# Column sums and the product with phi in 32-column strips, one transposed load of v dropped, three split pairs fewer, all steps reordered

## The chip, the cores and the metric

One core of one Trainium2 chip runs the whole kernel. The metric is the device time of one launch in microseconds (us), the median of three runs. TensorE (PE in the profile) multiplies, VectorE (DVE) and ScalarE (ACT) do the elementwise work, GpSimd (POOL) raises four small tiles to a power, and SyncE (SP) issues every DMA, one after the other, in its own queue.

## The reference

Two stages, everything in fp32. For each of B = 4 batches, column-normalised attention: q and k (5056 x 256) are divided by the norms of their columns, s = kn.T @ qn / tau is a 256 x 256 matrix, and a softmax over its rows gives a; the output of the stage is v @ a.

```
qn = q / (np.linalg.norm(q, axis=1, keepdims=True) + 1e-06)
kn = k / (np.linalg.norm(k, axis=1, keepdims=True) + 1e-06)
s = kn.transpose(0, 2, 1) @ qn / tau
a = softmax over the last axis of s
x = (v @ a).reshape(B * N, D)
logits = x @ phi                      # phi: 256 x 32
slot_input = softmax(logits, over rows).T @ x
h = relu(slot_input @ w1[e]);  slot_out = h @ w2[e]      # 8 experts, 4 slots each
out = softmax(logits, over the 32 slots) @ slot_out
```

The second stage is a soft mixture of experts over all 20224 rows at once: its first softmax runs over the rows of all four batches, so nothing of the experts can start before the last batch's logits are there.

## The kernel before, in words

**Pieces.** q and k come in 40 units of 1 MB (`raw0` to `raw39`, ten per batch, `load_qk`), v in 20 pieces of 1 MB (`v0` to `v19`, `load_v`). The logits need v transposed; each half (p, m) of a piece is either loaded in transposed form from a second copy in memory (`load_vt`, 0.5 MB, the pairs in the set `LT`) or turned on TensorE by four transposes per half of it (`turn`, L373, eight per pair (p, m)) and copied out by ScalarE (`turned`). Expert weights are 16 loads of 1 MB (`load_w1`, `load_w2`). The output is 20 MB, stored as ten halves of 0.5 MB and fifteen wholes of 1 MB (`store`).

**Scores.** Per unit there are four blocks j of 128 rows. `score` (L237) multiplies k.T q of a block into the batch's S, in one of two forms. Without a split the fp32 operands go in as they are: 4 matmul instructions per block (two per half m). If the pair (u, k) of blocks is in the set `SPLIT`, ScalarE copies it to a rounded high part (`cast`, L202), VectorE subtracts to get the low part (`low`, L207), and the block takes 6 cheaper instructions. ScalarE also squares every unit and VectorE adds the squares up (`add`), for the norms.

**Per batch**, in this order: `att_sums` folds the sum of squares to one tile a of 128 x 512; `att_cols` (L262) multiplies it by ones on TensorE so that the 512 column sums lie on partitions; `att_rn` copies them out on VectorE; `att_pow` takes the root on POOL; `att_norm` the reciprocal; `att_dg` (ScalarE) builds two diagonal matrices, and `att_row` (L296) multiplies ones by them so that each partition holds the row of q's norms; `att_scale`, `att_exp`, `att_turn`, `att_back` make a and its transpose; `att_phi` (L342) multiplies by phi; `att_m` (ScalarE) scales the product to M. With M, `logits` (L393) makes the logits of a piece of v straight from the transposed v, in four strips of 32 output partitions; `exps`, `weights`, `gather` do the row softmax and the weighted sum of v, group by group; `finish_fold` (L520) turns that sum by a matmul with the identity, and `finish_slots` multiplies by a.

**The end.** After the last `gather`, `last_slots` and `last_back` give the slot input; `up`, `relu`, `flip_h`, `down` are the experts, in two column halves h of the output. `down(r, h, f)` (L703) of the first half needs the four loads w2(k, 0), that of the second half the four w2(k, 1). `o_copy`, `o_fold`, `o_back` (L721 to L733) bring one half of the slot output into place, then `out_mul` (L740), `out_evict` and `store` make the output; the first ten stores are half ones.

**What sets the order.** Every call is entered in a list `plan`; the list `ORDER` then says, by hand, in which order all 992 calls are emitted. Each engine runs its own instructions strictly in that order, and SP its DMAs. All large tiles share 22 buffers of 1 MB; `HOME` says which tile lies in which buffer, so a load waits on SP for the last reader of the buffer's tile before it, and every load behind it waits too. `WAKE` dummy matmuls (L784) run on TensorE before the first data is there.

Of the kernel before, what the change touches and what calls it, by code (L numbers as in the profile page):

```python
# [8 lines left out]
F32 = mybir.dt.float32  # L9
F32R = mybir.dt.float32r  # L10
AF = mybir.ActivationFunctionType
ALU = mybir.AluOpType
# [8 lines left out]
WAKE = 9  # L21
# [4 lines left out]
SPLIT = {(u, 0) for u in range(1, NU) if u not in (1, 2, 3, 17, 20, 27, 31)} | {(u, 1) for u in (2, 5, 14, 24, 26, 27, 31, 33, 35, 37, 39)}  # L26
LT = {(p, 0) for p in (0, 2, 3, 4, 5, 6, 7, 8, 9, 11, 12, 13, 15, 18, 19)} | {(p, 1) for p in (0, 3, 6, 9, 12, 15)}
GR = {b: (3, 2) for b in range(B)}
HOME = {
# [74 lines left out]
def colnorm_attention_soft_moe(  # L104
# [157 lines left out]
    def att_cols(b):  # L262
        mp = bank(X0, f"nn{b}")
        a = sqs[b * UB][:, 0].rearrange("p x c -> p (x c)")
        for i in range(4):
            pe.matmul(mp[:, i : i + 1], a[:, P * i : P * i + P], ones[:, 0:1], start=True, stop=True)  # L266
# [829 lines left out]
```

## Time and profile before

| | |
|---|---|
| three runs | 276.80, 277.48, 277.49 us; median 277.48 us |
| the profiled execution | 277.06 us, of which 275.3 us are the span from first to last instruction |
| mean granted clock of TensorE | 0.939 of full |
| busy share of the span | PE 92%, DVE 86%, ACT 71%, POOL 3% |
| DMA | 111.44 MB moved, of it 90.08 MB read and 20.97 MB written |

The span is cut into 40 equal slices of 6.88 us in the page; a digit is the busy share of a slice in tenths. In the rows, a group is one line of the kernel on one engine, with its count, its total and the mean duration of one instruction. Matmuls overlap, so the time that a step takes on TensorE is read from start to start, as in the chain of waits, not from the mean duration of one.

### The profile page before, as it was taken

The numbers are of one execution on the slowest core, as the hardware profiler recorded it, in microseconds if no ns is written. First come the engines' busy times: TensorE is split into PE (matmuls) and PEld (weight loads), VectorE is DVE, ScalarE is ACT, GpSimd is POOL, SyncE is SP. The second block draws the span as 40 slices with busy tenths as digits, with TensorE's granted clock in tenths as the row PEclk, the third lists the DMA queues.
The fourth block names the chain that finished last, engine by engine and source line by source line (L and its number), as shares of the span: only waits on it lengthen the run. The fifth ranks groups of instructions, "written<-read, shape, count | busy, mean of one in ns | idle before, by whom it ended". The sixth has DMA issues, their size and how long they took to land.

```text
span 275.3 us, 6127 instructions
## 1 busy us (share of the span) xinstructions
PE 254.6 (92%) x2494; PEld 212.6 (77%) x2494; DVE 236.8 (86%) x349; ACT 195.5 (71%) x285; POOL 7.5 (3%) x12
## 2 busy tenths in 40 slices
PE   8999999999999999999999999999999988678730
PEld 8889998999998896997898978866555878457520
DVE  1599999999999999999999997887989879988630
ACT  3898989798899689899998783886416247353430
POOL 1000002000002000020000001000000000000000
PEclk9999999999999999999999999999999999855755
DMA  7999999999999999999999999999999789999995
GB/s 283 432 424 410 422 426 415 420 417 419 419 417 420 412 422 421 416 415 417 412 419 418 416 417 419 417 416 420 421 415 420 300 332 388 418 418 412 420 421 246
DMA packets 17883, 111.44 MB, mean 405 GB/s; under 512 B 2112, under 2 KB 2112, under 8 KB 6592
## 3 DMA queue, kind: packets, MB, share of 16 engines
q1 hardware_dynamic: 17856, 111.06, 98.0%
q8 instruction: 19, 0.31, 0.4%
q14 instruction: 8, 0.07, 0.1%
HBM read 90.08 MB, written 20.97 MB: 403 GB/s over the span
## 4 chain that ended last, share of the span: by engine, by line
PE 87%; DVE 6%; ACT 3%; issue 1%; DVEq 0%; ACTq 0%
PE S L255 46%; PE op_None L750 8%; PE L L403 7%; PE G L503 7%; PE vTp L376 6%; PE op L750 3%; PE O L711 2%; DVE o L774 2%; ACT o L772 2%; PE wake L787 2%; PE Mp L347 1%; PE nn L266 1%; DVE nat L630 1%; DVE cm L627 1%; PE sp L549 1%; PE gt L525 1%
## 5 line engine op out<-in xcount | busy, mean ns | idle before, releaser
L235 DVE TENSOR_TENSOR sq<-sq,sq 128x1024 f32<-128x1024 f32 (+1 forms) x61 | 81.3, 1356 | 8.4 <-ACT sq L220 8.0
L220 ACT ACTIVATE sq<-raw 128x2048 f32<-128x2048 f32 (+1 forms) x40 | 74.7, 1889 | 6.5 <-DMA raw<-in_qk_dram 4.8
L255 PE MATMUL S<-hl 128*128 128x256 f32 x516 | 71.5, 291 | 0.0
L255 PE MATMUL S<-raw 128*128 128x256 f32 (+1 forms) x296 | 66.9, 384 | 0.0
L255 PEld LDWEIGHTS S<-hl 128*128 128x128 f32 x516 | 65.2, 191 | 1.0
L255 PEld LDWEIGHTS S<-raw 128*128 128x128 f32 (+1 forms) x296 | 53.7, 192 | 8.1 <-issue 1.5
L209 DVE TENSOR_TENSOR hl<-raw,hl 128x1024 fp32r<-128x1024 f32 x43 | 51.6, 1219 | 0.7 <-ACT hl L204 0.7
L204 ACT CAST hl<-raw 128x1024 fp32r<-128x1024 f32 x43 | 44.0, 1048 | 6.1 <-PE S L255 2.5
L750 PE MATMUL op_None<-so,lg 32*128 32x256 f32 x240 | 26.4, 525 | 6.0 <-ACT o L772 4.1
L772 ACT COPY o<-op_None 128x512 f32<-128x512 f32 x30 | 15.8, 594 | 18.2 <-PE op_None L750 17.9
L750 PEld LDWEIGHTS op_None<-so,lg 32*128 32x128 f32 x240 | 19.6, 251 | 11.6 <-ACT o L772 6.3
L381 ACT COPY x<-vTp 128x512 f32<-128x512 f32 x38 | 21.5, 593 | 9.3 <-PE vTp L376 8.8
L774 DVE COPY o<-op_None 128x512 f32<-128x512 f32 x30 | 19.0, 678 | 8.0 <-PE op_None L750 8.0
L376 PE MATMUL vTp<-ident,v 128*128 128x128 f32 x152 | 21.6, 276 | 0.0
L403 PE MATMUL L<-x,M 128*32 128x256 f32 (+1 forms) x320 | 20.3, 379 | 0.0
L376 PEld LDWEIGHTS vTp<-ident,v 128*128 128x128 f32 x152 | 17.3, 143 | 2.8 <-issue 2.5
L503 PE MATMUL G<-v,dn 128*32 128x256 f32 x320 | 19.1, 381 | 0.0
L503 PEld LDWEIGHTS G<-v,dn 128*32 128x32 f32 x320 | 10.8, 110 | 5.9 <-issue 0.7
L403 PEld LDWEIGHTS L<-x,M 128*32 128x32 f32 x320 | 9.8, 109 | 6.2 <-issue 0.8
L750 PE MATMUL op<-so,lg 32*128 32x128 f32 x160 | 9.6, 315 | 2.0 <-ACT o L772 1.4
L750 PEld LDWEIGHTS op<-so,lg 32*128 32x128 f32 x160 | 7.7, 197 | 4.4 <-ACT o L772 2.7
L772 ACT COPY o<-op 128x256 f32<-128x256 f32 x20 | 6.4, 378 | 6.3 <-PE op L750 6.3
(112 smaller groups left out, 233.0 us busy)
## 6 DMA issues: line engine op xcount, KB each, us to landing
raw<-in_qk_dram SPq DMA_DIRECT2D x37, 1024.0 KB, 12.5
v<-in_v_dram SPq DMA_DIRECT2D x20, 1024.0 KB, 11.1
w<-in_moe_w_dram SPq DMA_DIRECT2D x16, 1024.0 KB, 17.5
out_dram<-o SPq DMA_DIRECT2D x15, 1024.0 KB, 7.5
x<-in_vt_dram SPq DMA_DIRECT2D x17, 512.0 KB, 10.2
out_dram<-o SPq DMA_DIRECT2D x10, 512.0 KB, 3.7
raw<-in_qk_dram SPq DMA_DIRECT2D x3, 768.0 KB, 10.0
x<-in_vt_dram SPq DMA_DIRECT2D x4, 480.0 KB, 11.9
```

The lines of the kernel that those rows point to most:

```text
L204: act.copy(hl[:, :, 0::2, :], raws[u][:, 2 * k : 2 * k + 2])
L209: dve.tensor_tensor(hl[:, :, 1::2, :], raws[u][:, 2 * k : 2 * k + 2], hl[:, :, 0::2, :].bitcast(F32), op=ALU.subtract)
L220: act.activation(sq_tile(u)[:, :n], raws[u][:, :n], AF.Square)
L235: dve.tensor_tensor(a[:, lo:hi], a[:, lo:hi], s[:, lo:hi], op=ALU.add)
L255: pe.matmul(sm, w, x, start=first[bb], stop=False, skip_group_check=True)
L376: pe.transpose(tp[:, P * jj : P * jj + P], vs[p][:, 4 * h + jj, P * m : P * m + P], ident)
L381: act.copy(x[:, h * UT : h * UT + UT], tps[p, h, m])
L403: pe.matmul(L[S * g : S * g + S, :n, :], M[:, m, :], x[:, :n, S * g : S * g + S], start=m == 0, stop=m == 1,)
L503: pe.matmul(gp[S * g : S * g + S, :C], dn[:, x, j, :], vt[:, j, :], start=x == 0 and j < G, stop=x == n - 1 and j >= G,)
L750: pe.matmul(ops[b, p, hf, g][:, h, :], cT[b][S * g : S * g + S, 4 * i : 4 * i + 4, :].rearrange("s j t -> s (j t)"), so[S * g : S * g + S] ...
L772: act.copy(dst, src)
L774: dve.tensor_copy(dst, src)
```

## The change

1. `WAKE` falls from 9 to 6 (each is two instructions).
2. `SPLIT` has 40 pairs in place of 43 (26 first pairs for 32, and 14 second pairs for 11). `LT` loses (11, 0): that half of v11 is turned on TensorE, no longer loaded.
3. `att_cols` no longer takes a as the stationary operand against one column of ones (8 instructions). It takes 32 columns of ones as the stationary operand and streams a, 128 columns wide, into four strips of 32 partitions. The sums then lie along the rows; `att_rn` turns them with a VectorE transpose in blocks of 32 x 32 out of PSUM, in place of its copy, and `att_pow` reads one column of each block.
4. `att_dg` is gone; `att_row` streams the identity past the broadcast norms, twice 128 columns in place of once 256.
5. `att_phi` streams the transposed a, 64 columns wide, past phi as a stationary operand of 32 columns, into four strips; a new step `att_flip` (VectorE transpose of 128 x 64 out of PSUM) turns the result for `att_m`, which now reads SBUF.
6. For batches 0 to 2 the turning matmul `finish_fold` becomes a TensorE transpose (`finish_turn`); batch 3 is as before.
7. `HOME` and `ORDER` are new throughout.

```diff
-WAKE = 9
+WAKE = 6
-SPLIT = {(u, 0) for u in range(1, NU) if u not in (1, 2, 3, 17, 20, 27, 31)} | {(u, 1) for u in (2, 5, 14, 24, 26, 27, 31, 33, 35, 37, 39)}
-LT = {(p, 0) for p in (0, 2, 3, 4, 5, 6, 7, 8, 9, 11, 12, 13, 15, 18, 19)} | {(p, 1) for p in (0, 3, 6, 9, 12, 15)}
+SPLIT = {(u, 0) for u in range(1, NU) if u not in (2, 3, 5, 6, 16, 17, 18, 19, 21, 22, 23, 24, 27)} | {(u, 1) for u in (2, 5, 7, 13, 14, 15, 22, 23, 27, 31, 33, 35, 37, 39)}
+LT = {(p, 0) for p in (0, 2, 3, 4, 5, 6, 7, 8, 9, 12, 13, 15, 18, 19)} | {(p, 1) for p in (0, 3, 6, 9, 12, 15)}
...
     def att_cols(b):
-        mp = bank(X0, f"nn{b}")
-        a = sqs[b * UB][:, 0].rearrange("p x c -> p (x c)")
-        for i in range(4):
-            pe.matmul(mp[:, i : i + 1], a[:, P * i : P * i + P], ones[:, 0:1], start=True, stop=True)
+        mp = bank(X0, f"nn{b}")[:, :P]
+        a = sqs[b * UB][:, 0].rearrange("p x (m g s) -> p g (x m) s", m=2, g=G)
+        for g in range(G):
+            pe.matmul(mp[S * g : S * g + S, :], ones[:, :S], a[:, g], start=True, stop=True)
         st[b]["mp"] = mp
     def att_rn(b):
+        nt = bpool.tile([P, P], F32, tag="ob", name=f"nt{b}", bufs=2)
+        dve.transpose(nt, st[b]["mp"])
+        st[b]["nt"] = nt.rearrange("p (i s) -> p i s", s=S)[:, :, 0]
+
+    def att_pow(b):
         rn = bpool.tile([P, 4], F32, tag="rn", name=f"rn{b}")
-        dve.tensor_copy(rn, st[b]["mp"][:, 0:4])
+        pool.tensor_tensor(rn, st[b]["nt"], half, op=ALU.pow)
         st[b]["rn"] = rn
...
     def att_row(b):
         rq = bank(X0, f"rq{b}")
-        pe.matmul(rq[:, :C], ones, st[b]["dg"], start=True, stop=True)
+        for i in range(2):
+            pe.matmul(
+                rq[:, P * i : P * i + P], st[b]["rn"][:, i : i + 1].broadcast_to([P, P]), ident, start=True, stop=True
+            )
...
     def att_phi(b):
...
+        mps = bank(X0, f"Mp{b}")[:, : 2 * S]
+        aT = st[b]["aT"].rearrange("p n (m g s) -> p n g m s", m=2, g=G)
+        for n in range(2):
+            for g in range(G):
+                pe.matmul(mps[S * g : S * g + S, :], phi_sb[:, n, :], aT[:, n, g], start=n == 0, stop=n == 1)
         st[b]["mps"] = mps
+    def att_flip(b):
+        mt = bpool.tile([P, 2, S], F32, tag="mt", name=f"mt{b}")
+        dve.transpose(mt.rearrange("p m s -> p (m s)"), st[b]["mps"])
+        st[b]["mt"] = mt
...
+    def finish_turn(b):
+        gs = st[b]["gs"]
+        gt = bank(X0, f"gt{b}")[:, :C].rearrange("p (m s) -> p m s", m=2)
+        for m in range(2):
+            pe.transpose(gt[:, m, :], gs[:, P * m : P * m + P], ident)
```

**The order of the loads on SP**, as far as the prediction speaks of it. The first units come in the order 0 to 6, 9, 8, 7, 17, 19, 10, 13, 16, 12, ... before and 0 to 6, 9, 19, 7, 12, 8, 10, 13, 18, 17, 14, 20, v1, 16, ... after. The last loads are, written w1 e and w2(k, h):

- before: w1 1, w1 4, vt(15, 1), w1 2, v15, vt(19, 0), w1 3, w1 7, w1 0, w2(0, 0), w1 5, w2(3, 0), w2(2, 0), w2(1, 0), w2(0, 1), w2(1, 1), w2(3, 1), and last of all w2(2, 1);
- after: w2(2, 0), w2(3, 0), w1 0, v15, w1 6, w1 3, w1 2, w1 7, w1 1, w1 4, w1 5, w2(0, 0), w2(1, 0), w2(0, 1), w2(1, 1), w2(2, 1), w2(3, 1).

Before and after, `down(0, 1, 0)`, the first step of the second half, stands on TensorE right before the first `o_fold`.

## Rows read from the trace of the kernel before

**Rows 1.** The page: busy share of each engine, clock and DMA in 40 slices.

```profile
PE   8999999999999999999999999999999988678730
...
DVE  1599999999999999999999997887989879988630
...
PEclk9999999999999999999999999999999999855755
DMA  7999999999999999999999999999999789999995
GB/s 283 432 424 410 422 426 415 420 417 419 419 417 420 412 422 421 416 415 417 412 419 418 416 417 419 417 416 420 421 415 420 300 332 388 418 418 412 420 421 246
```

**Rows 2.** The page: the DMA queue of all loads and stores; packets, MB, share.

```profile
q1 hardware_dynamic: 17856, 111.06, 98.0%
```

**Rows 3.** The chain that ended last, in order of time: start us, us, what.

```profile
1.04 4.21 PE wake L787 x18
...
44.02 0.79 PE nn L266 x8
...
62.60 0.87 PE vTp L376 x8
...
75.42 2.15 PE S L255 x18
77.57 0.81 PE Mp L347 x8
...
79.29 1.73 PE S L255 x8
...
94.31 1.00 PE L L403 x16
...
128.76 0.45 PE gt L525 x4
...
222.41 1.89 PE O L711 x64
```

**Rows 4.** Two stretches: us, then busy PE, PEld, DVE, ACT, POOL, clock, DMA share, GB/s.

```profile
120.00:160.00 40.00, 40.00 (x395) 35.82 (x395) 39.29 (x56) 35.46 (x54) 0.00 (x0) 1.00 1.02 417
160.00:200.00 40.00, 40.00 (x510) 28.69 (x508) 33.37 (x84) 26.27 (x68) 1.01 (x1) 1.00 1.02 418
```

**Rows 5.** The same view of the two stretches around the first stores.

```profile
217.00:221.00 4.00, 3.87 (x98) 2.84 (x92) 2.73 (x6) 1.45 (x5) 0.00 (x0) 1.00 0.52 212
225.00:229.00 4.00, 3.48 (x73) 3.10 (x77) 3.70 (x10) 2.98 (x11) 0.00 (x0) 1.00 0.65 260
```

**Rows 6.** Groups of VectorE by line and form: busy us, mean ns, idle before.

```profile
L209 DVE TENSOR_TENSOR hl<-raw,hl 128x1024 fp32r<-128x1024 f32 x43 | 51.6, 1219 | 0.7 <-ACT hl L204 0.7
...
L651 DVE STREAM_TRANSPOSE lg<-nat 128x512 f32<-128x512 f32 x3 | 2.1, 702 | 0.0
...
L651 DVE STREAM_TRANSPOSE lg<-nat 128x256 f32<-128x256 f32 x5 | 2.0, 420 | 0.0
...
L271 DVE COPY rn<-nn 128x4 f32<-128x4 f32 x4 | 0.6, 157 | 0.0
```

**Rows 7.** Timeline of SP: the last three weight loads, and the first stores.

```profile
195.40 5.29 SPq L666 DMA_DIRECT2D w<-in_moe_w_dram  x3
219.54 10.89 SPq L782 DMA_DIRECT2D out_dram<-o  x9
```

**Rows 8.** The line of the w2 loads: time from issue to landing.

```profile
DMA to landing us min/median/max: 17.3/19.9/19.9
```

**Rows 9.** TensorE at L255 alone, in the stretch behind the dummy matmuls.

```profile
5.04:6.32 1.28, 1.27 (x3) 1.02 (x4) 1.00 1.05 442
```

**Rows 10.** Timeline: start us, us, what; two ScalarE waits for loads, and the fold.

```profile
5.65 1.91 ACT L220 ACTIVATE sq<-raw 128x2048 f32<-128x2048 f32 x1 [3.43 <-DMA raw<-in_qk_dram]
...
10.55 1.05 ACT L204 CAST hl<-raw 128x1024 fp32r<-128x1024 f32 x1 [0.57 <-DMA raw<-in_qk_dram]
...
216.37 0.49 PE L727 MATMUL fo<-ob,fold 128*128 128x128 f32 x2
```

More of the change, by code (lines that the diff above doesn't have):

```diff
@@ L262, in att_cols @@
     def att_cols(b):
-        mp = bank(X0, f"nn{b}")
-        a = sqs[b * UB][:, 0].rearrange("p x c -> p (x c)")
-        for i in range(4):
-            pe.matmul(mp[:, i : i + 1], a[:, P * i : P * i + P], ones[:, 0:1], start=True, stop=True)
+        mp = bank(X0, f"nn{b}")[:, :P]
+        a = sqs[b * UB][:, 0].rearrange("p x (m g s) -> p g (x m) s", m=2, g=G)
+        for g in range(G):
+            pe.matmul(mp[S * g : S * g + S, :], ones[:, :S], a[:, g], start=True, stop=True)
         st[b]["mp"] = mp
     def att_rn(b):
+        nt = bpool.tile([P, P], F32, tag="ob", name=f"nt{b}", bufs=2)
+        dve.transpose(nt, st[b]["mp"])
+        st[b]["nt"] = nt.rearrange("p (i s) -> p i s", s=S)[:, :, 0]
+    def att_pow(b):
         rn = bpool.tile([P, 4], F32, tag="rn", name=f"rn{b}")
-        dve.tensor_copy(rn, st[b]["mp"][:, 0:4])
+        pool.tensor_tensor(rn, st[b]["nt"], half, op=ALU.pow)
         st[b]["rn"] = rn
-    def att_pow(b):
-        rn = st[b]["rn"]
-        pool.tensor_tensor(rn, rn, half, op=ALU.pow)
     def att_norm(b):
@@ L288, in att_rk @@
         st[b]["rk"] = rk
-    def att_dg(b):
-        dg = bpool.tile([P, C], F32, tag="gts", name=f"dg{b}")
-        for i in range(2):
-            act.mul(dg[:, P * i : P * i + P], ident, st[b]["rn"][:, i : i + 1])
-        st[b]["dg"] = dg
     def att_row(b):
         rq = bank(X0, f"rq{b}")
-        pe.matmul(rq[:, :C], ones, st[b]["dg"], start=True, stop=True)
+        for i in range(2):
+            pe.matmul(
+                rq[:, P * i : P * i + P], st[b]["rn"][:, i : i + 1].broadcast_to([P, P]), ident, start=True, stop=True
+            )
         st[b]["rq"] = rq
@@ L342, in att_phi @@
     def att_phi(b):
-        mps = bank(X0, f"Mp{b}")
-        aT = st[b]["aT"]
-        for m in range(2):
-            for n in range(2):
-                pe.matmul(
-                    mps[:, S * m : S * m + S],
-                    aT[:, n, P * m : P * m + P],
-                    phi_sb[:, n, :],
-                    start=n == 0,
-                    stop=n == 1,
-                )
+        mps = bank(X0, f"Mp{b}")[:, : 2 * S]
[3 more added lines that the diff above has]
+                pe.matmul(mps[S * g : S * g + S, :], phi_sb[:, n, :], aT[:, n, g], start=n == 0, stop=n == 1)
         st[b]["mps"] = mps
+    def att_flip(b):
+        mt = bpool.tile([P, 2, S], F32, tag="mt", name=f"mt{b}")
+        dve.transpose(mt.rearrange("p m s -> p (m s)"), st[b]["mps"])
+        st[b]["mt"] = mt
     def att_m(b):
-        mps = st[b]["mps"]
+        mt = st[b]["mt"]
         M = bpool.tile([P, 2, S], F32, tag="M", name=f"M{b}", bufs=2)
         for m in range(2):
-            act.mul(M[:, m, :], mps[:, S * m : S * m + S], st[b]["sm"][:, m : m + 1])
+            act.mul(M[:, m, :], mt[:, m, :], st[b]["sm"][:, m : m + 1])
         st[b]["M"] = M
@@ L521, in finish_fold @@
         gs = st[b]["gs"]
-        w = P if b < B - 1 else S
-        gt = bank(X0, f"gt{b}")[:, : 2 * w].rearrange("p (m s) -> p m s", m=2)
+        gt = bank(X0, f"gt{b}")[:, : 2 * S].rearrange("p (m s) -> p m s", m=2)
         for m in range(2):
-            pe.matmul(gt[:, m, :], gs[:, P * m : P * m + P], ident if b < B - 1 else run["fw"], start=True, stop=True)
+            pe.matmul(gt[:, m, :], gs[:, P * m : P * m + P], run["fw"], start=True, stop=True)
+        st[b]["gt"] = gt
+    def finish_turn(b):
[3 more added lines that the diff above has]
+            pe.transpose(gt[:, m, :], gs[:, P * m : P * m + P], ident)
         st[b]["gt"] = gt
@@ L856, in colnorm_attention_soft_moe @@
                 if gi:
-                    at(k + 0.77, finish_fold, b)
+                    at(k + 0.77, finish_turn if b < B - 1 else finish_fold, b)
                     at(k + 1.02, finish_mul, b)
@@ L870, in colnorm_attention_soft_moe @@
         at(k + 1.55, att_norm, b)
-        at(k + 1.56, att_dg, b)
         at(k + 1.57, att_rk, b)
@@ L880, in colnorm_attention_soft_moe @@
         at(k + 2.72, att_phi, b)
+        at(k + 2.775, att_flip, b)
         at(k + 2.78, att_m, b)
@@ L887, in colnorm_attention_soft_moe @@
     at(NU - 0.2, att_norm, 3)
-    at(NU - 0.19, att_dg, 3)
     at(NU - 0.18, att_rk, 3)
@@ L934, in colnorm_attention_soft_moe @@
     tail(4.05, att_phi, 3)
+    tail(4.1, att_flip, 3)
     tail(4.1, att_m, 3)
@@ L960, in colnorm_attention_soft_moe @@
     tail(12.2, finish_evict, 2, gl)
-    tail(12.78, finish_fold, 2)
+    tail(12.78, finish_turn, 2)
     tail(13.1, finish_mul, 2)
```

133 rows, old and new, of tables (HOME, ORDER) are left out of this document.

## The prediction, made before the changed kernel ran

> **What bounds the kernel now.** I read the page's slices first [rows 1]: TensorE, VectorE and the DMAs all stand at nine tenths or more from the second slice to about the 26th, and only the DMAs go on so to slice 31. Three resources are full at once, so the question is not who is busy but what the end hangs on. The single DMA queue carries 98.0% of what sixteen engines could carry in the whole span [rows 2]. It is below that in three places: in the first slice, in slices 32 to 34 (300, 332 and 388 GB/s against some 418), and at the very end [rows 1]. The dip is where the loads run out and the first stores begin. A finer view puts numbers on it: from 217 to 221 us the DMAs are busy for 0.52 of the time, from 225 to 229 us for 0.65, so they lose 4 x 0.48 + 4 x 0.35 = 3.3 us there [rows 5]. Behind that the queue is full again until the last store.
>
> So the end is: the time at which the stores can begin and follow on each other, plus some 50 us of writing at a fixed rate (20.97 MB at 418). The kernel gets faster by what the first stores come earlier, up to the 3.3 us of the dip plus what is saved in bytes, and not by more. The first store is issued at 219.54 us [rows 7]. The last of the eight w2 loads is issued at 195.40 + 5.29 - 0.33 = 200.4 us and lands 19.9 us later, at 220.3 [rows 7, 8]: loads and stores meet nearly head to tail. Ahead of the stores the chain of waits runs almost wholly over TensorE, from the dummy matmuls at 1.04 us to the last gather at about 200 us (pieces of it in [rows 3]), and in no part of 120 to 200 us is TensorE idle; VectorE is busy for 39.3 of 40 us up to 160 us and for 33.4 of 40 after it [rows 4].
>
> **The change part by part.** All times are from start to start.
>
> Split pairs. 18 instructions of split scores take 2.15 us, 8 of unsplit ones 1.73 [rows 3]. A pair is 12 of the first, 1.43 us, or 8 of the second, 1.73: each pair dropped costs TensorE 0.30, three cost +0.9. VectorE loses three `low` of 1.22 us, -3.7 [rows 6]. ScalarE loses three casts and the diagonal matrices and gains two copies; it is busy for 35 and 26 of 40 us [rows 4], and I cost that at nothing, since TensorE's work hides it. Without that cover the sum would still be a saving.
>
> The dropped load. 0.524 MB at 418 GB/s [rows 4] is -1.25 us of the queue, and since all loads before it are back to back, every later load comes earlier by that. The eight transposes that replace it take 0.87 on TensorE [rows 3].
> The Trainium skill, "DMA: Bandwidth & Descriptors", section Specifications, gives one core a limit of about 358 GB/s from memory; by it the dropped load would be worth 1.46 us. The queue here moves 417 to 418 for 40 us on end, so the measurement decides.
>
> Column sums. 8 instructions take 0.79 [rows 3]. The new ones are again 8, 128 columns wide, in strips of 32. No row has them; the experts' second product has that shape: 64 in 1.89, 0.030 each, and the logits, 256 columns wide in strips, take 16 in 1.00, 0.063 each [rows 3]. So 0.24 to 0.50; I take 0.24, the same shape: -0.55 per batch, -2.2 for four.
>
> Product with phi. 8 instructions, 0.81 [rows 3], become 16 of 64 columns. If they go as the 128-column ones do, 0.48; at half of that, by columns, 0.24. I take 0.48, as nothing shows an instruction that short: -0.33 each, -1.3 for four.
>
> Turn of the gathered sum. Four instructions, 0.45, become two transposes of 0.11 (eight take 0.87) [rows 3]: -0.23, three times, -0.7. The row of q's norms: once 256 columns or twice 128, equal; the lost diagonal matrices shorten a wait in which TensorE has other scores.
>
> VectorE's new transposes. Those of 256 and 512 columns take 0.42 and 0.70 [rows 6], so 0.28 at 128 and 0.21 at 64 by the line through both. All those read SBUF and the new ones PSUM, which no row shows; twice that is my upper bound, the line my value. With the copy of 0.157 that goes [rows 6] it is 4 x (0.28 - 0.16 + 0.21) = +1.3, at most +3.3. VectorE's sum: -3.7 + 1.3 = -2.3, and -0.4 at the upper bound.
>
> The start. 18 dummies fill 1.04 to 5.25 [rows 3]; three of the unsplit scores behind them take 0.43 each [rows 9], twice the 0.216 of later ones: the pace of the lower of its levels (1.2 of 2.4 GHz), though the profile gives the granted clock as 1.00 there. Six dummies fewer in instructions free 1.3 us of that stretch, at half pace and with a wait for the rest of the first unit, which lands at 5.6 [rows 10]. Worth -0.5; if the clock rises later by as much, nothing.
>
> TensorE's sum: +0.9 + 0.9 - 2.2 - 1.3 - 0.7 - 0.5 = -2.9. Not all of it arrives. Units land 2.5 us apart and cannot be met earlier: the third lands at 10.5 [rows 10], and after the change TensorE is there at 10.4 or earlier. Adding up the new order against a landing every 2.5 us, it has to wait at units 2, 3, 19 and 16, by 0.2 to 0.3 each: +1.0 in all, between 0.4 and 1.6. So the slot input comes earlier by 1.9 on TensorE and by 2.3 on VectorE's count; the later one rules: -1.9.
>
> The gate behind it. `down(0, 1, 0)` stands right before the fold at 216.37 [rows 10] and needs w2(1, 1), the third from last load before and after. It lands at 195.40 + 19.9 = 215.3 now [rows 7, 8] and at 214.05 after. With 16 instructions of 0.03 and the copy that feeds it the fold can start at 214.6 or so, 1.7 earlier and no more. `down(0, 0, 0)` meets the same gate, two loads ahead, at 209.05.
>
> The new order. I looked at each load for the last reader of its buffer. The two w2 loads that move up wait for the scores of units 39 and 35, in place of later readers; a w2 load now lies in the queue for 17.3 to 19.9 us before it lands [rows 8], so the DMAs have other loads to do while SP waits there. The stores keep their order, and from the tenth on they wait for the DMAs, not for the engines.
>
> **The sum.** The stores can begin 1.25 earlier for the bytes alone, up to 1.7 by the gate, 1.9 by the engines. I take 1.5. The profiled execution took 277.06 us (span 275.3), so 275.5 in its terms; the median of the runs stands 0.4 above it, which gives **276.0 us**. About 0.3% (0.8 us) is what a measurement of this kernel can tell from no change.
>
> **The rivals.**
> - The engines' gain does not arrive (the PSUM transposes at their upper bound leave VectorE -0.4, and it is full up to 160 us). Then the loads end 1.25 us earlier and the DMAs wait for the same first store: 277.5. For it: 39.3 of 40 [rows 4]. Against it: three `low` fewer. Chance 0.20.
> - The dip closes too. If the stores come 3 us earlier, the gaps at 217 and 225 us [rows 5] shrink as well: 277.5 - 3 = 274.5, and 272.9 at the floor of 1.25 + 3.3. It needs the fold ahead of its load; only the order of the stores behind the fold could give it. Chance 0.12.
> - Slower, by a new wait on VectorE. `att_flip` makes VectorE wait for TensorE's product with phi, where ScalarE waited before. While it waits, `low` and `add` of the next units are queued behind it, and TensorE's split scores behind these. Four flips at 1 us each turn VectorE's -2.3 into +1.7: 279.2. It decides from 0.6 us per flip on. For it: VectorE has no slack; against it: adding up the rows in the new order, VectorE comes to the four flips 0 to 5 us after the product is there. Chance 0.15.
> - TensorE's clock falls ahead of the stores. The granted clock is 1.00 from 120 to 200 us [rows 4], with transposes between scores throughout; each 5 us at the lower level would cost 2.5, hence 278.5. The Trainium skill, "TensorE: Matmul & The Clock Gate", Part 4, says that transposes do not count as TensorE being busy in the way matmuls do, and the change adds some; by that rule the clock would be at risk. The rows bear out none of it so far. Chance 0.03.
>
> **How the numbers follow.** My forecast has 0.50. Faster are it and the second rival, 0.62; the first is no change, 0.20; slower are the last two, 0.18. The range leaves out the lower half of the second rival and most of the slower ones: 274.4 to 277.7.
>
> **What would show it.** Right: the column sums at 0.25 and the product with phi at 0.5 in the chain; the last load landing near 219.0; the first store issued near 218, and a dip of about 3 us. Wrong: a first store at 219.5 or later; VectorE idle before line `att_flip`; DMA below 410 GB/s before 210 us; or a dip that is gone.

## The result, and the profile after

The changed kernel takes 279.43 us (median of 5 runs, 278.9 to 279.96); the kernel before takes 277.48 in the same comparison (5 runs, 276.8 to 278.47). The ratio is 1.0062, with a 95% interval of 1.0039 to 1.0085: slower by 0.6%, where 276.0 had been forecast. The profiled execution took 279.43 us, its span is 277.6.

The page after: the 40 slices of TensorE, VectorE, clock and DMA, which answer to [rows 1], and the queue's line, which answers to [rows 2].

```profile
PE   8999999999999999999999999999999889678700
...
DVE  1699989999996999999999899877898789997710
...
PEclk9999999999999999999999999999999999966965
DMA  7999999999699999999999999999999789999995
GB/s 284 427 423 415 421 423 418 421 419 417 230 425 420 414 420 415 419 410 421 414 418 419 421 407 417 421 421 418 421 417 420 290 329 387 415 412 415 420 423 233
...
q1 hardware_dynamic: 17712, 110.54, 96.9%
```

Ahead of the first stores one number differs clearly from before: the eleventh slice, 230 GB/s where [rows 1] have 419. The dip at the first stores is there as it was (290, 329, 387 against 300, 332, 388). The queue's share fell from 98.0% to 96.9% [rows 2]: 0.52 MB fewer of 111.06 explain about 0.5 points of that; the rest is time in which the queue was dry.

Finer stretches around the eleventh slice (us; busy PE, PEld, DVE, ACT, POOL; clock, DMA share, GB/s):

```profile
66.00:70.00 4.00, 4.00 (x26) 3.67 (x25) 3.96 (x6) 3.90 (x6) 0.00 (x0) 1.00 1.02 418
70.00:72.00 2.00, 2.00 (x16) 1.77 (x15) 1.97 (x3) 2.00 (x5) 0.00 (x0) 1.00 0.25 102
72.00:74.00 2.00, 2.00 (x17) 1.98 (x16) 2.00 (x2) 2.00 (x3) 0.00 (x0) 1.00 0.52 92
74.00:78.00 4.00, 4.00 (x25) 3.61 (x24) 3.96 (x7) 4.00 (x5) 0.00 (x0) 1.00 1.02 417
```

The DMAs lose 2 x 0.75 + 2 x 0.48 = 2.5 us here while all three engines are full. So nothing shows on the engines, and a reader who looks only for idle engines passes it by. Who held the queue stands in the view of waits, asked for SP alone from 58 to 76 us (engine, line, tile, released by what: us in total, times, longest):

```profile
SPq L161 <- DVE sq L234: 10.0, 1, 10.0
```

And the timeline of SP and, behind it, of VectorE in that stretch:

```profile
61.53 0.33 SPq L145 DMA_DIRECT2D raw<-in_qk_dram  x1
71.87 0.33 SPq L161 DMA_DIRECT2D x<-in_vt_dram  x1
72.25 0.42 SPq L159 DMA_DIRECT2D x<-in_vt_dram  x1
72.77 0.37 SPq L153 DMA_DIRECT2D v<-in_v_dram  x1
73.24 1.40 SPq L145 DMA_DIRECT2D raw<-in_qk_dram  x3
...
70.59 3.61 DVE L234 TENSOR_TENSOR sq<-sq,sq 128x1024 f32<-128x1024 f32 x3
```

SP issues nothing from 61.9 to 71.87 us. L161 is `load_vt(4, 0)`. It writes into x4, whose buffer (14) held the squares of unit 16 before. Their last reader is `add(16, 0, 2)` on VectorE, the first of the three additions at 70.59. The new order does that addition late and issues the load early. SP works in order, so five other loads wait behind it (vt 0, v 2, raw 25, 29 and 22); they go out one behind the other as soon as it does. What had been issued before lasts the DMAs for some 8 us, to about 70; then they are dry until the loads issued from 71.87 on come through.

What the queue lost there is still missing at the end. The line of the chain's shares, first of the kernel before and then of the changed one, in which the DMAs now have a part; then TensorE's last steps ahead of the first stores (H and O are the experts' two products, fo the first fold) and SP's first stores, which answer to [rows 7, 10], and the stretches that answer to [rows 5]:

```profile
PE 87%; DVE 6%; ACT 3%; issue 1%; DVEq 0%; ACTq 0%
PE 52%; DMA 26%; DVE 11%; issue 3%; ACT 2%; SPq 0%; DVEq 0%; ACTq 0%
...
207.57 1.92 PE L679 MATMUL H<-w,slT 128*32 128x512 f32 x14 [0.45 <-DMA w<-in_moe_w_dram]
...
215.07 2.86 PE L713 MATMUL O<-w,hT 128*32 128x128 f32 x91
218.64 0.42 PE L713 MATMUL O<-w,hT 128*32 128x128 f32 x5 [0.72 <-issue]
218.99 0.49 PE L729 MATMUL fo<-ob,fold 128*128 128x128 f32 x2
...
221.59 11.47 SPq L784 DMA_DIRECT2D out_dram<-o  x9
...
217.00:221.00 4.00, 3.28 (x84) 2.27 (x74) 2.78 (x6) 0.54 (x3) 0.00 (x0) 1.00 0.72 293
221.00:225.00 4.00, 3.77 (x100) 2.94 (x94) 3.20 (x9) 2.17 (x8) 0.00 (x0) 1.00 0.68 276
225.00:229.00 4.00, 3.48 (x98) 2.85 (x90) 3.07 (x7) 1.31 (x6) 0.00 (x0) 1.00 0.76 301
```

TensorE waits for a w1 tile, and it pauses once more right ahead of the fold; the last w2 load lands at 222.42 (before: 220.24), the fold comes at 218.99 (216.37), the first store is issued at 221.59 (219.54). These 2.05 us are close to the 1.95 by which the medians differ.

The pause ahead of the fold is easily taken for a wait for the tile w2(1, 1), and it is not one. That tile landed at 217.47 by the DMA's record, and the first product that needs it is recorded at 217.51. TensorE stops only in the middle of this group of products, from 217.93 to 218.64, for nothing that the profile shows (`issue`). The kernel before has a pause at the same place of TensorE's stream, ahead of the 4034th instruction that the trace records, and there it falls behind the fold, into products of the first output that need no such tile (the view of waits of the weight loads, 217.5 to 218.2 us):

```profile
PEld op L750 <- issue: 0.3, 1, 0.3
```

What both have in common is a transfer of 16 KB of instructions (queue q8, the fifteenth in each trace): here it ended at 217.27 and TensorE went on 1.38 us later, in the kernel before it ended at 216.54 and TensorE went on 1.44 us later. In none of the fourteen traces does that instruction come less than 1.29 us behind the end of this transfer. So the record points to the instructions and not to the tile; no run was made to test it.

The changed operations themselves did what they were meant to. Groups of TensorE and VectorE by line and form (busy us, mean ns, idle before); the first two lines are of the kernel before, the others of the changed one:

```profile
L347 PE MATMUL Mp<-few_sb,aT 128*128 128x32 f32 x32 | 4.0, 267 | 0.0
L266 PE MATMUL nn<-ones,sq 128*128 128x1 f32 x32 | 3.8, 240 | 0.0
...
L344 PE MATMUL Mp<-aT,few_sb 128*32 128x64 f32 x64 | 1.7, 224 | 0.0
L265 PE MATMUL nn<-sq,ones 128*32 128x128 f32 x32 | 1.7, 278 | 0.0
L527 PE MATMUL gt<-ident,gs 128*128 128x128 f32 x6 | 1.3, 291 | 0.0
...
L270 DVE STREAM_TRANSPOSE nt<-nn 128x128 f32<-128x128 f32 x4 | 1.2, 308 | 0.0
L349 DVE STREAM_TRANSPOSE mt<-Mp 128x64 f32<-128x64 f32 x4 | 1.0, 248 | 1.4 <-PE Mp L344 1.4
```

The kernel before has 3.8 us for the column sums, 4.0 for the product with phi and, in the same view, 1.9 for the turns: 5.0 us less on TensorE in all. VectorE waited for the product with phi for 1.4 us in all four batches together.

### The profile page after: what moved, and what is told of

It reads as the page before. It is cut to its first block, busy times and chain, and to the rows that moved or that the text cites. A ratio compares the mean times of both kernels' runs of the same rounds, so it can differ in the third digit from the quotient of the medians.

```text
span 277.6 us, 6149 instructions
## 1 busy us (share of the span) xinstructions
PE 251.9 (91%) x2518; PEld 205.1 (74%) x2518; DVE 235.6 (85%) x350; ACT 191.6 (69%) x276; POOL 8.4 (3%) x12
## 3 DMA queue, kind: packets, MB, share of 16 engines
q1 hardware_dynamic: 17712, 110.54, 96.9%
## 4 chain that ended last, share of the span: by engine, by line
PE 52%; DMA 26%; DVE 11%; issue 3%; ACT 2%; SPq 0%; DVEq 0%; ACTq 0%
PE S L254 29%; DMA raw<-in_qk_dram 14%; DMA w<-in_moe_w_dram 12%; PE vTp L372 4%; PE op_None L752 4%; DVE o L776 3%; PE O L713 3%; PE L L399 3%; PE op L752 3%; DVE sq L234 3%; PE G L499 2%; PE H L679 1%; DVE hl L208 1%; ACT o L774 1%; PE hTp L695 1%
## 5 line engine op out<-in xcount | busy, mean ns | idle before, releaser
L254 PE MATMUL S<-raw 128*128 128x256 f32 (+1 forms) x320 | 75.1, 388 | 0.6 <-DMA raw<-in_qk_dram 0.4
L254 PE MATMUL S<-hl 128*128 128x256 f32 x480 | 69.5, 294 | 0.2 <-DVE hl L208 0.2
L254 PEld LDWEIGHTS S<-raw 128*128 128x128 f32 (+1 forms) x320 | 57.4, 192 | 10.1 <-DMA raw<-in_qk_dram 2.4
L254 PEld LDWEIGHTS S<-hl 128*128 128x128 f32 x480 | 61.6, 190 | 2.1 <-issue 0.5
L208 DVE TENSOR_TENSOR hl<-raw,hl 128x1024 fp32r<-128x1024 f32 x40 | 47.7, 1211 | 6.9 <-ACT hl L203 6.9
L203 ACT CAST hl<-raw 128x1024 fp32r<-128x1024 f32 x40 | 41.1, 1045 | 9.4 <-DMA raw<-in_qk_dram 4.8
L377 ACT COPY x<-vTp 128x512 f32<-128x512 f32 x40 | 22.5, 585 | 9.1 <-PE vTp L372 7.4
L752 PE MATMUL op_None<-so,lg 32*128 32x256 f32 x240 | 24.8, 462 | 4.2 <-DVE lg L653 1.3
L752 PEld LDWEIGHTS op_None<-so,lg 32*128 32x128 f32 x240 | 18.3, 221 | 10.2 <-ACT o L774 3.2
L372 PE MATMUL vTp<-ident,v 128*128 128x128 f32 x160 | 22.4, 275 | 0.0
```

The lines of the kernel that those rows point to most:

```text
L203: act.copy(hl[:, :, 0::2, :], raws[u][:, 2 * k : 2 * k + 2])
L208: dve.tensor_tensor(hl[:, :, 1::2, :], raws[u][:, 2 * k : 2 * k + 2], hl[:, :, 0::2, :].bitcast(F32), op=ALU.subtract)
L254: pe.matmul(sm, w, x, start=first[bb], stop=False, skip_group_check=True)
L372: pe.transpose(tp[:, P * jj : P * jj + P], vs[p][:, 4 * h + jj, P * m : P * m + P], ident)
L377: act.copy(x[:, h * UT : h * UT + UT], tps[p, h, m])
L752: pe.matmul(ops[b, p, hf, g][:, h, :], cT[b][S * g : S * g + S, 4 * i : 4 * i + 4, :].rearrange("s j t -> s (j t)"), so[S * g : S * g + S] ...
```

## The experiments

Twelve kernels ran, each against the kernel before on the same chip. The order of the steps is a list of numbers in the code; the diffs give the steps' names.

**1. The load moved.** The changed kernel, SP's order:

```diff
-('load_vt', 4, 0)
 ('load_vt', 0, 1)  ('load_v', 2)  ('load_qk', 25)  ('load_qk', 29)  ('load_qk', 22)
+('load_vt', 4, 0)
```

> The changed kernel with one step moved: SP issues the load of the halves of vt 4 behind five loads that it stood ahead of (vt 0, v 2, raw 25, raw 29, raw 22). Nothing else differs. Theory 1 (in the changed order this load waits on SP for a square sum that VectorE adds late, from 61.9 to 71.9 us, the loads behind it wait too, the 16 DMA engines run dry for 2.4 us, and the DMA bounds the kernel from there): the dry stretch near 70 us goes, the last w2 tile lands some 2.4 us earlier (222.4 to about 220), and the time falls from 279.4 to about 277.0 (276.5 to 277.7). Theory 2 (the time is set by VectorE and by TensorE waiting for it in the new forms): 279.4, no change. Theory 3 (only the bytes count): 279.4, no change, the DMA being as busy in sum.

276.97 us, ratio to the kernel before 0.9979 (0.9962 to 0.9997): the 2.4 us are back, as theory 1 had it, and theories 2 and 3 fall. The stretches that were dry:

```profile
70.00:72.00 2.00, 2.00 (x16) 1.80 (x15) 2.00 (x2) 2.00 (x6) 0.00 (x0) 1.00 1.01 412
72.00:74.00 2.00, 2.00 (x16) 1.92 (x15) 1.97 (x3) 2.00 (x3) 0.00 (x0) 1.00 1.01 420
```

The last w2 tile lands at 219.47, 2.95 earlier than in the changed kernel and 0.8 earlier than before the change. The fold, at 216.41, is no earlier than before the change [rows 10].

**2. The addition moved.** The changed kernel, VectorE's order; SP's is untouched:

```diff
 ('add', 16, 2, 4)
+('add', 16, 0, 2)
 ('att_rk', 0)  ('add', 19, 2, 4)  ('low', 15, 0)  ('low', 11, 0)  ...  ('low', 15, 1)
-('add', 16, 0, 2)
```

> The changed kernel with one step moved on VectorE alone: the addition of the two squared halves of unit 16, for which the load of vt 4 waits on SP, is done nine steps earlier in the common list, right behind another addition of that unit's neighbour. SP's order is that of the changed kernel. Theory 1 (SP's queue blocked by one wait): the wait of some 10 us on SP shrinks to a few us or none, the DMA stays fed, and the time falls to about 277.0 (276.5 to 278.0), as when the load itself is moved. Theory 2 (VectorE and the forms): 279.4, since VectorE has the same work. If this one falls less than the one with the load moved, the addition still comes too late.

277.26 us, ratio 0.9996 (0.9977 to 1.0016). The load's wait for VectorE fell from 10.0 us to 1.1, in the same view (the list of steps is two lines longer here, so the load stands on L163):

```profile
SPq L163 <- DVE sq L236: 1.1, 1, 1.1
```

The load is issued at 63.40 us in place of 71.87, and the two stretches that were dry have 403 and 421 GB/s.

So it is the pair of places, the early load and the late addition, that cost the time; moving either gives it back. With this, the cause of the slowdown is shown. The other runs ask why the remaining gain is 0.5 us and not 1.5.

**3. The forms alone.** The new forms in the order, splits, buffers and loads of the kernel before; `att_flip` right ahead of `att_m`, `finish_turn` in the place of `finish_fold`, no `att_dg`.

> The new forms of the column sums, of the product with phi and of the fold alone, in the order of the kernel before: its split pairs, its list of halves that are loaded, its 9 wake-up instructions and its buffers; no load is dropped or moved. The step that built the diagonal matrix is out, and the new turning step on VectorE stands right ahead of the scaling that reads it. Theory 1 (the DMA gates most of the kernel, and TensorE's savings find a way to the end only where no load stands between): 0.0 to -0.8 us against the kernel before, so 276.7 to 277.5. Theory 2 (TensorE's chain bounds, as the prediction took it): the forms' -4.2 us arrive nearly whole, 273.5 to 274.5. Rival: VectorE's turning step is waited for and its wait costs, 278 to 279.

278.65 us, ratio 1.0039 (1.0017 to 1.0061): slower, as only the rival had it. TensorE is busy for 5 us less (254.6 to 249.6), and the time grows by 1.1 us by the ratio. VectorE and then TensorE around the second batch's turning step show the place:

```profile
121.45 2.32 DVE L237 TENSOR_TENSOR sq<-sq,sq 128x1024 f32<-128x1024 f32 x2
123.68 1.22 DVE L211 TENSOR_TENSOR hl<-raw,hl 128x1024 fp32r<-128x1024 f32 x1
124.82 0.24 DVE L352 STREAM_TRANSPOSE mt<-Mp 128x64 f32<-128x64 f32 x1
...
122.01 0.43 PE L347 MATMUL Mp<-aT,few_sb 128*32 128x64 f32 x16
125.47 0.64 PE L402 MATMUL L<-x,M 128*32 128x256 f32 x8 [1.30 <-ACT M L359]
```

The product is done at 122.44. The turning step of 0.24 us stands in VectorE's queue behind additions and a low part and starts 2.4 us later; the logits wait for it.

**4. The forms, the turning step earlier.** As 3, and the work that stood ahead of the turning step on VectorE goes behind it:

```diff
-('att_sums', 1, 2)  ('att_sums', 1, 1)
 ...
 ('att_flip', 0)
+('att_sums', 1, 2)  ('att_sums', 1, 1)
 ...
-('low', 33, 1)
 ...
 ('att_flip', 1)
+('low', 33, 1)
```

> The run of the new forms alone on the order of the kernel before, with VectorE's turning step of blocks 0 and 1 moved ahead of the work that it stood behind (the two halvings of block 1's squares, 2 us; one low part, 1.2 us). In the run before, these two stood 2.5 and 2.4 us behind the product with phi that they turn, and the logits waited 1.3 us each. Theory A (the forms are slower here because the turning step is queued on VectorE: its place costs what the forms save): the two waits of TensorE at the logits fall by 1 to 2 us in sum, and the time falls from 278.65 to 276.7 to 277.8. Theory B (the forms cost in themselves, by their narrow matmuls): 278.4 to 278.9.

277.30 us, ratio 0.999 (0.9968 to 1.0011): theory A. The place of two instructions of 0.24 us is worth 1.3 us. What is left is that the forms alone are worth nothing in the old order. From 120 to 160 us:

```profile
120.00:160.00 40.00, 39.11 (x409) 33.82 (x408) 39.33 (x58) 34.79 (x50) 0.00 (x0) 1.00 1.02 418
```

Beside [rows 4], TensorE now idles for 0.9 us of these 40, and VectorE (39.33 us here, 39.29 before) and the DMAs are as full as they were. The products that make the slot input begin at 200.84, 0.26 earlier than before the change (201.10), so nearly all of the 5.0 us had gone by then. Time taken off one of three full resources became waiting for the other two. Behind that point the profiled execution also has the granted clock at 0.50 from 202.6 to 206.0 us, which that of the kernel before has not; what that costs at the end is not shown.

**5. The forms and the dropped load, in the old order.** As 3, without the load of the first half of vt 11:

```diff
+('turn', 11, 0, 0, 'T0')  ('turn', 11, 1, 0, 'X1')
 ...
+('turned', 11, 0, 0)  ('turned', 11, 1, 0)
 ...
-('load_vt', 11, 0)
```

> The same as the run of the forms alone, and the first half of vt 11 is turned on TensorE (two turns, two copies on ScalarE) and not loaded. Theory 1 (the DMA gates the end): the load's 0.5 MB less lets the later loads land about 1.2 us earlier, and the time falls by 0.6 to 1.2 us against the forms alone, to about 276. Theory 2 (TensorE's chain bounds): two turns more cost 0.9 us against the forms alone. Theory 3 (only the bytes count, the forms are worth nothing): -1.25 us against the kernel before.

279.25 us, ratio 1.0072 (1.0044 to 1.0101): 0.6 above the forms alone, though the two intervals overlap. Theories 1 and 3 fall, and theory 2 is nearest. The last w2 tile lands at 219.39, 1.5 us earlier; TensorE comes to its fold at 219.90, 2.4 later. Part of these 2.4 us is the clock: in this profiled execution (280.13 us, 0.9 above the median) it stood at 0.50 from 204.8 to 208.2 us, and at 1.00 in that of experiment 3.

**6. The dropped load alone**, in the kernel before; the diff is that of 5.

> The kernel before with one load fewer: the first half of vt 11 is turned on TensorE (two turns) and copied by ScalarE, and not loaded; nothing else differs. Theory 1 (the end is set by TensorE's chain from the last scores to the first fold, the loads landing early enough): the later loads land some 1.2 us earlier, TensorE comes to its first fold 0.5 to 1.0 us later, and the time is 277.5 to 278.3. Theory 3 (the bytes set the time): 276.0 to 276.3.

279.05 us, ratio 1.0051 (1.0026 to 1.0076), above theory 1's range and far from theory 3. In the profiled execution (278.02 us, the fastest of twelve) the loads do land 1.2 us earlier (the last at 219.05), the fold comes at 217.94, 1.6 later, and between the two the DMAs run dry:

```profile
217.00:221.00 4.00, 4.00 (x110) 2.98 (x106) 3.57 (x6) 1.01 (x4) 0.00 (x0) 1.00 0.19 70
```

The share is 0.19 where [rows 5] have 0.52, with TensorE full. Why the drop costs more than the 0.87 us of its turns is not shown.

**7. The load moved, and wake-up products.** In the run of experiment 1 TensorE's granted clock fell ahead of the experts' first product:

```profile
199.00:201.00 2.00, 2.00 (x17) 2.00 (x17) 1.28 (x8) 0.00 (x0) 0.00 (x0) 0.96 1.03 410
201.00:203.00 2.00, 2.00 (x11) 0.74 (x14) 1.93 (x5) 0.19 (x1) 0.00 (x0) 0.50 1.01 422
203.00:205.00 2.00, 2.00 (x20) 0.56 (x16) 2.00 (x2) 0.22 (x1) 0.00 (x0) 0.68 1.01 422
```

The clock column, third from the right, goes to 0.50, the lower of its levels (1.2 of 2.4 GHz), behind a wait of 0.61 us for VectorE at 198.3 and a run of products 32 columns wide. The edit:

```diff
+    tail(23.29, wake, 3, T0)
     tail(23.3, finish_fold, 3)
```

> The changed kernel with the load of vt 4 moved as before, and three more wake-up products (six matmuls of 128 columns into a bank that is free there) on TensorE right ahead of the last fold's turning, where TensorE had waited 0.61 us for VectorE at 198.3 us before its granted clock fell from 1.00 to 0.50 for some 3.5 us (200.9 to 204.4). Theory 1 with the clock (the load moved gives the DMA back its 2.4 us, and this fall of the clock then takes some 1.7 us of the 16 us in which TensorE works without a pause up to the first fold): the clock stays at 1.00 up to 225 us, the first fold comes at about 215.0 where it came at 216.4, and the time falls from 277.0 to 275.2 to 276.0. Rival (the last w2 tiles, which land at 214.5 and 219.5, hold the stores): the fold comes earlier, the DMA's dry stretch moves with it, and the time stays at 276.7 to 277.2.

276.65 us, ratio 0.9964 (0.9943 to 0.9984). The clock stays at 1.00 there, and the first three groups of the experts' products end at 206.46 in place of 208.13; but the fold, at 216.17, is only 0.2 earlier. TensorE gives the time up again in a pause:

```profile
215.61 0.63 PE L715 MATMUL O<-w,hT 128*32 128x128 f32 x11 [0.99 <-issue]
```

It lies in `down(0, 1, 0)`, the group that needs w2(1, 1). By the DMA's record that tile landed at 214.28; the group's first product is recorded at 214.32, and the next one at 215.61. This is the pause described above, at the same place of the stream: the transfer of instructions ended at 214.22, 1.39 us before TensorE went on. The time is nearest to the rival's (0.05 below its range), but the tile that the rival names had come.

Whether the wake-up products held the clock is not shown either. The changed kernel has the same wait of 0.61 us and the same narrow products, and its clock stayed at 1.00. Of the profiled executions, one of each kernel, the clock falls here in four of the nine without these products (experiments 1, 2, 4 and 5) and in none of the five with them (7, 8, 9, 11 and 12).

**8. The fold first.** The run of 7, TensorE's order:

```diff
-('down', 0, 1, 0)
 ('o_copy', 0)  ...  ('o_fold', 0)
+('down', 0, 1, 0)
```

> The run with the load moved and three wake-up products, with one step more moved on TensorE: the one product group of the second half of the output weights that stood ahead of the first fold is done behind it. In the run before, that group began at 214.08 us and ended at 216.24 because its w2 tile came only then, and the fold stood behind it. Theory 1 (the first fold, which lets the stores start, waits for a w2 tile that it does not need): the fold comes at 214.7 to 215.0 in place of 216.2, the first store 0.5 to 1.5 us earlier, and the time falls from 276.65 to 275.2 to 276.2. Rival (what feeds the stores is set by the product groups that still follow, which wait for the same tile): 276.4 to 276.8.

276.17 us, ratio 0.9957 (0.9941 to 0.9973): faster than the kernel before by 0.43% and than the changed one by 1.0%. The fold comes at 214.88, the first store at 218.38. The move takes the fold out from behind the group with the tile and the pause; the expectation lays all of that time to the tile, the record only its part up to 214.28. The intervals of 1, 7 and 8 overlap, so of the 0.8 us between 1 and 8 neither the sum (0.6 by the ratios) nor the share of each is sure; the gain over the kernel before is.

**9. The first output ahead too.** The run of 8, TensorE's order:

```diff
-('down', 0, 1, 0)
 ('o_back', 0)
-('down', 0, 1, 4)
 ('out_mul', 0, 1, 0, 1)
+('down', 0, 1, 0)  ('down', 0, 1, 4)
```

> As the run with the fold first, and the first output's products also stand ahead of the two product groups of the second half that wait for that w2 tile, so that TensorE meets the tile only after it has made something to store. Theory 1: the first store comes 1.5 us earlier than in the run with the wake-up products (at about 217.2), and the time falls to 275.0 to 276.0. Rival (the DMA has the loads to bring until 219.2 anyway, and the stores can't be fed before TensorE has more outputs): 276.4 to 276.8.

276.33 us, ratio 0.9957 (0.9941 to 0.9974): no different from 8, though the first store is issued at 217.53, 0.85 earlier. It lies between the two ranges. The rival's reason is nearly right: the second store, at 219.36, is only 0.25 earlier.

**10. The fold first, in the kernel before.** The same move as in 8.

> The kernel before with the same step moved: the product group of the second half that stands ahead of the first fold goes behind it. There it began at 215.76 us and took its 0.62 us, so that its tile had come. Theory 1 (TensorE's chain sets the first fold there, not the tile): the fold can come 0.4 us earlier at most, and waits for VectorE's copy instead: -0.3 to +0.1 us against the kernel before. Rival (the tile holds it there too): -1 us.

277.56 us, ratio 1.0006 (0.9989 to 1.0022): nothing, by theory 1. There the tile was not late, and the pause stands behind the fold. The fold comes at 216.19, behind a wait of 0.43 for the copy.

**11. The old forms in the new order.** The run of 7 with the old column sums, product with phi, diagonal matrix and turn.

> The run with the load moved and three wake-up products, with the old forms of the column sums, of the product with phi and of the fold's turning put back (and the diagonal matrix made again), in the changed order with its splits, its dropped load and its buffers. Theory 1 (VectorE and the DMA are full up to 160 us, so TensorE's time saved by the new forms is mostly turned into waiting): 276.5 to 277.5, that is 0 to +0.8 us against the run with the new forms. Theory 2 (TensorE's sum bounds, as the prediction took it; the forms save it some 3.3 us): 279 to 280.

283.67 us, ratio 1.0242 (1.0217 to 1.0267): 7.0 above the run of 7, beyond both theories. Part of it is where this run makes the diagonal matrices, which the new order has no place for:

```profile
PE rq L299 <- ACT dg L294: 3.4, 2, 2.3
```

With the 5.0 us of the forms that makes 8.4 us more for TensorE, of which 7.0 arrive. TensorE frees buffers later, SP waits for them, and seven slices of the DMA, from the 11th to the 26th, fall below 400 GB/s. How much the forms alone would cost here stays open.

**12. The dropped load put back**, in the run of 8: SP issues it behind `load_v(13)`, and the two turns and copies are out.

> The run with the fold first, with the change's dropped load put back: the first half of vt 11 is loaded again, issued on SP behind v 13, and the two turns on TensorE with their two copies on ScalarE are out. Theory 1 (in this order, too, TensorE's chain up to the first fold and the stores behind it set the end, as the same drop made the kernel before slower): TensorE comes to the fold some 0.9 us earlier, the loads land 1.2 us later, and the time is 275.3 to 276.2, not above the 276.17 without the load. Rival (with the turning the DMA has become the gate, and its bytes count): the w2 tiles land 1.2 us later, and the time is 276.6 to 277.4.

277.47 us, ratio 1.0009 (0.999 to 1.0028): 1.3 above the run of 8, as the rival has it (0.07 above its range). The last w2 tile lands at 220.62 (219.43), and TensorE comes to its fold not earlier but later, at 216.07 (214.88). In the new order the load is worth about its bytes. That rests on all runs of both: the two profiled executions (276.51 us here, 276.69 in 8) do not show the difference.

## Why the prediction was wrong

- **The step that failed: "The new order: I looked at each load for the last reader of its buffer."** The prediction names the w2 loads and says nothing of `load_vt(4, 0)`, for which it does not hold. That load and the turned half of vt 4 share the tile x4, and the buffer had held the squares of unit 16 before; their last addition, late on VectorE, is a reader that the prediction has no wait for. A wait of 10.0 us on SP and 2.5 us of dry queue came of it; taking it out moved the time by 2.46 us (279.43 to 276.97). The condition under which such a wait is harmless, that the DMAs have other loads to do, I had argued for the end of the kernel, where a load lies 20 us in the queue [rows 8]; at 62 us the backlog was 8.
- **The forms.** By busy time, column sums -2.1 us (I had -2.2), product with phi -2.3 (-1.3), turns -0.6 (-0.7); from start to start, as I had counted, -2.0, -2.1 and -0.8. The first and the last are right, the second too small: I had taken 0.48 us for its 16 instructions, and from their start to the next instruction's they take 0.25 to 0.36. Of the column sums only the difference is right: a new one takes 0.33 to 0.36, not 0.24, and the old ones took 0.81 to 0.88, not 0.79. VectorE's turning steps took 308 and 248 ns (I had 280 and 210): near the line, far from the upper bound.
- **"Not all of it arrives."** Right for the changed order once the blocked load is out: the products that make the slot input begin at 199.38 in experiment 1 and at 201.10 before the change, 1.7 earlier where I had 1.9. In the changed kernel itself they begin at 200.88, 0.2 earlier. That 1.7 and 1.9 lie so close is in part luck: I had taken off 1.0 us for waits for the early units, and TensorE idles for 0.35 us from 6 to 44 us in experiment 1. For the forms alone it is far too mild: in the old order none of their gain arrives (experiment 4), as VectorE and the DMAs are full beside TensorE. That comes close to the first rival, at 0.20.
- **The dropped load, -1.25 us.** Right in the new order (-1.3, experiment 12), wrong as a rule: in the old order the same drop costs 1.4 us by its ratio (experiment 6).
- **The gate.** Named rightly, and mis-sized. The fold was to start 0.55 us behind the landing of w2(1, 1); it started 1.5 behind it in the changed kernel (217.47 to 218.99) and 1.9 in experiment 7. The tile has no part in the excess, as the first product that needs it is recorded 0.04 us behind its landing; the excess is the pause inside the group, 1.0 and 1.3 us from one product's start to the next, for which the prediction has no term.
- **The dip.** It stayed, as forecast. In the changed kernel it is 4 x (0.28 + 0.32 + 0.24) = 3.4 us.
- **The sum.** Without the blocked load, and with two small mends at the gate (7, 8), the kernel stands 1.1 us below the kernel before (0.5 without them), where I had 1.5. The mechanism was there; one wait on SP outweighed it.
- **The rivals.** The slowdown that came was none of mine. VectorE waited for the product with phi for 1.4 us, not four times 1 us. Its opposite, the turning step late in VectorE's queue, is real (1.3 us between 3 and 4), but not in the changed order. The clock's fall, at 0.03, did come in experiment 1, behind narrow products and a wait; the changed kernel, with the same products and the same wait, shows none, so what brings it on stays open. The rule of the Trainium skill that I had weighed ("TensorE: Matmul & The Clock Gate", Part 4, on transposes not counting as TensorE being busy) is neither borne out nor refuted by these runs: in the changed kernel, with eight transposes of vt more, the clock is at 1.00 until long past the first stores.
- **What would show it.** "DMA below 410 GB/s before 210 us" and "a first store at 219.5 or later" were signs named for wrong; both came. A third, VectorE idle before `att_flip`, came small, with 1.4 us.

## What to carry to other kernels

When an order is changed, list for each queue of DMAs the instruction that every load waits for, by buffer and not by tile name, and hold the time at which that instruction ends against the load's place in the queue and the backlog ahead of it: one load that waits longer than the backlog stops all the loads behind it, and no engine shows it at that time. Where three resources are full at once, a saving on one is worth what the order lets the other two make of it. The same edit (a load dropped for two turns) was worth -1.3 us in one order and cost 1.4 in the other.

## What the hardware showed that was not expected

- The first product that waits for a weight tile is recorded 0.04 us behind the tile's landing (217.47 to 217.51 in the changed kernel, 214.28 to 214.32 in experiment 7). The pause that follows there stands at a fixed place of TensorE's instructions and ends 1.38 and 1.39 us behind a transfer of 16 KB of them; in the kernel before, without a tile, it is 1.44 us.
- One wait of 0.61 us with 32-column products around it was followed by some 3.5 us at half the granted clock in experiment 1 and by none in the changed kernel. With three 128-column products in the place of the wait no profiled execution had the fall (five kernels).
- Products in strips went by columns down to 64: from the first one's start to the next instruction's, sixteen of 64 columns took 0.25 to 0.36 us and, where nothing was waited for, eight of 128 columns 0.33 to 0.36 (changed kernel).
